# The way from attention into the experts: first weights outside the order that is kept, gates in half steps, and a later scan

## The chip, the cores and the metric

The kernel runs on one core of a Trainium2 chip. Its engines are named as in the profile: PE (TensorE, with PEld for its weight loads), DVE (VectorE), ACT (ScalarE), POOL (GpSimd) and SP (SyncE, which here only issues DMAs). The metric is the device time of one execution in microseconds (us).

## The reference

An attention with a mask from clusters, and a layer of eight experts behind it, whose gates are made by eight rounds of row and column normalisation. Cut to what matters (4 batches, 8 heads, 768 positions of 64; 3072 tokens of 512, 8 experts with 1024 hidden columns):

```python
# attention
q_assign = argmax(q_n @ c_n.T); k_assign = argmax(k_n @ c_n.T)
scores = where(q_assign[:, None] == k_assign[None, :], scale * q @ k.T, -1e9)
attn = exp(scores - max(scores)); attn = attn / (sum(attn) + 1e-9)
x = attn @ v                      # (4, 8, 768, 64) -> (3072, 512)
# experts
P = exp(x @ w_gate - max(x @ w_gate))
for _ in range(8):
    P /= P.sum(1, keepdims=True) + 1e-9
    P /= P.sum(0, keepdims=True) + 1e-9
    P *= N / E
for e in range(E):
    out += P[:, e:e + 1] * (maximum(x @ w1[e], 0) @ w2[e])
```

## The kernel before

**Attention** works through 32 pairs of a batch and a head. Each is a set of generator processes that ask a `Planner` for an engine and a time; the planner simulates the engines with estimated durations and writes the instructions out in the order of its simulated times. Its `LATENCY` and the estimates in the `yield` lines decide that order. `keep_order()` (L76) then pins it: each instruction traced so far gets an edge to the one before it on its engine, so that the scheduler cannot move it. `self.last` holds the last pinned instruction per engine, and the next one is tied to it.

When a batch is complete, `out_batch(b)` (L916) stores its transposed output `xT` to `xd[b]` in memory (L918), and makes the gates' logits `lg` (L935 to L951). For batch 0 it also reduces `xT` to its largest entry `amx` (L286) and makes from it the power of two by which the experts' input is scaled (`input_scale`, its helper's lines L238 to L269); that scale is `sx`. Late in attention the inputs of batch 0 are loaded as four quarters `xqB` and split into two float16 parts, `xs` (L300 on ACT, L303 on DVE).

**The experts** are 128 items: four batches by eight experts by four quarters of the hidden columns (`NP2` = 4). The items of batch 0 come first, then the other batches; t counts the items. An item's first layer is seven products (m = 0 to 6) of six matmuls each (L1181), combined on DVE (u and c, L1209; hl, L1197) and ACT (L1194, L1214). The second layer (L1249 to L1251, o_ps) runs one item late, between the products. In the loop over m, single steps of other generators are issued behind each product: `sink` (the gates), `scanning`, `inputs` (the next batch's input), `making` (the weights), and the loop pins the order of it all with `keep_order()` at each m.

- `load_raw(idx)` (L1074, L1078) loads a quarter of an expert's w1 and w2, two tiles of 512 KB. `make_w` scales them on ACT (L1087, L1098), forms four sums and differences (L1096), casts to float16 on ACT (L1101, L1104, L1107) and subtracts for the low part (L1102, L1105, L1108), on POOL, for item 0 on DVE. During batch 0 the made weights `wa` and `wb` are stored to `wd` (L1113, L1114), and the other batches load them from there (L1119, L1120).
- `gates()` (L1022): largest logit over all (L1025, a transpose, L1030, then a matmul with ones at L1033), exp (L1036), then eight rounds. A round is the row sums (L1039 to L1042), the column sums (L1044), a yield, a matmul with ones over the partitions (L1047) and the division (L1049 to L1052).
- `scan(e)` takes the largest entry of the next expert's weights: eight loads of 512 KB into two tiles (L279, L283) and eight reductions (L286), of which each issues the load after the next. The weights' scale comes from it. The scan of expert 0 lies in attention.
- `next_x(b)`: the four `xqB` loads of the next batch (L1152), the four maxima (L286 again), the scale (L238 to L269), differences on POOL (L296), and splitting.

PE, DVE, ACT and POOL each take their instructions in order, and SP issues the DMAs in order: one that waits for its tile holds up those behind it.

Of the kernel before, what the change touches and what calls it, by code (L numbers as in the profile page):

```python
# [8 lines left out]
F32 = mybir.dt.float32  # L9
# [5 lines left out]
ALU = mybir.AluOpType  # L15
# [43 lines left out]
class Planner:  # L59
# [93 lines left out]
def attn_moe_kernel(  # L153
# [154 lines left out]
    with ExitStack() as actx:  # L308
# [607 lines left out]
        def out_batch(b):  # L916
            yield SP, 0.625
            nc.sync.dma_start(out=xd[b], in_=xts[b])  # L918
            ev["stored", b].set(plan, plan.copied(4.4))
            if b == 0:  # L920
                yield DVE, 3.3
                largest(amx, xts[b].rearrange("p c s -> p (c s)"))
                yield t_x
                yield from input_scale(b, amx, misc_tile, sm)
                t_x.put(plan)
                ev["xmax"].set(plan)

            NG, N = NT // 2, 2 * P
            yield t_x
            for c in range(NC):  # L930
                yield PE, 0.47, 0.107, 0.43
                if c == 0:
                    ps = misc_tile()
                for g in range(NG):
                    nc.tensor.matmul(  # L935
                        ps[g * Q : (g + 1) * Q, 0:N], wg[:, c, :], xts[b][:, c, g * N : (g + 1) * N], start=(c == 0), stop=(c == NC - 1)
                    )
            ev["batch", b].set(plan)
            yield DVE, 0.335
            gt = sm.tile([NG * Q, N], F32, name="gt", bufs=1)  # L940
            nc.vector.tensor_copy(gt, ps[0 : NG * Q, 0:N])
            t_x.put(plan)
            yield t_x
            yield PE, 0.25, 0.107, 0.1
            ps = misc_tile()
            for i in range(2):
                nc.tensor.transpose(
                    out=ps[:, i * NG * Q : (i + 1) * NG * Q], in_=gt[:, i * P : (i + 1) * P], identity=ident[0 : NG * Q, 0 : NG * Q]
                )
            yield DVE, 0.1  # L950
            nc.vector.tensor_copy(  # L951
                lg[:, b * NT : (b + 1) * NT, :].rearrange("p (g i) e -> p i g e", i=2),
                ps[:, 0 : 2 * NG * Q].rearrange("p (i g e) -> p i g e", i=2, e=Q)[:, :, :, 0:E],
            )
            t_x.put(plan)
# [67 lines left out]
    def gates():  # L1023
# [11 lines left out]
        nc.vector.tensor_scalar(out=gneg, in0=ps[:, 0:1], scalar1=-1.0, scalar2=None, op0=ALU.mult)  # L1035
        nc.scalar.activation(pr, lg, AF.Exp, bias=gneg)  # L1036
        for it in range(8):
            r = gs.tile([P, NTT], F32, name="rsum")
            nc.vector.tensor_reduce(out=r, in_=pr, axis=AX, op=ALU.add)  # L1039
            nc.vector.tensor_scalar(out=r, in0=r, scalar1=1e-9, scalar2=None, op0=ALU.add)  # L1040
# [5 lines left out]
            ps = h_tile()  # L1046
            nc.tensor.matmul(ps[:, 0:E], ones, c, start=True, stop=True)  # L1047
# [3 lines left out]
            nc.vector.tensor_scalar(out=c2, in0=c2, scalar1=float(B * S) / E, scalar2=None, op0=ALU.mult)
            nc.vector.tensor_tensor(out=pr, in0=pr, in1=c2.unsqueeze(1).broadcast_to([P, NTT, E]), op=ALU.mult)  # L1052


# [26 lines left out]
    def make_w(idx, wt, by=nc.gpsimd):  # L1081
# [22 lines left out]
        nc.scalar.copy(wa[:, 0, 3:7], S_)  # L1104
        by.tensor_tensor(out=wa[:, 1, 3:7], in0=S_, in1=wa[:, 0, 3:7], op=ALU.subtract)  # L1105
        yield
        nc.scalar.copy(wb[:, 0], r2)  # L1107
        by.tensor_tensor(out=wb[:, 1], in0=r2, in1=wb[:, 0], op=ALU.subtract)  # L1108
        yield

    def store_w(idx, wt):
        fa, fb = flat(*wt)
# [33 lines left out]
    def next_x(b):  # L1146
# [5 lines left out]
            nc.sync.dma_start(out=xq[o], in_=xd[b][:, k * KC : (k + 1) * KC, j * HB : (j + 1) * HB])  # L1152
        yield
        yield
        for i, o in enumerate(XQ):
            largest(am4[:, i : i + 1], xq[o].rearrange("p c s -> p (c s)"))
            yield
        for t, a, c in LESS["T2"]:
            less(t, a, c, nc.gpsimd)
        am = gs.tile([P, 1], F32, name="am")  # L1160
        nc.vector.tensor_reduce(out=am, in_=am4, axis=AX, op=ALU.max)
        for _ in input_scale(b, am, h_tile, gs):
            yield
        for o in XS:
            if o == "B21":
                for t, a, c in LESS[o]:
# [126 lines left out]

    made = {}
    begins = {begin(i): i for i in range(NI)}
    scan_at = {1: 0, 2: 2 * NP2 - 1, **{e: 2 * NP2 * (e - 1) - NP2 - 1 for e in range(3, E)}}
    sink, scanning, making, inputs = gates(), iter(()), iter(()), iter(())
    before = iter(())
    accs = {}
    load_raw(0)  # L1300
    load_raw(1)
    wt = made[0] = w_tiles(True)
    for _ in make_w(0, wt, nc.vector):
        pass
    t = 0
    for n, (b, e) in enumerate(order):
        if e == 0:
# [4 lines left out]
        for f2 in range(NP2):  # L1312
# [19 lines left out]
            hl = hp.tile([P, 2, S], F16, name="hl")  # L1332
            for m, _ in enumerate(layer1(wt, xs[b], hh, hl)):

                if m in (0, 3, 5):
                    step(sink)
                if m in (0, 3) or m in (2, 5) and 7 <= t < 11:
                    step(scanning)
                if m in (0, 2, 3, 5, 6):
                    step(inputs)  # L1340
                while rests:
                    rests.pop(0)()
# [43 lines left out]
```

## Time and profile before

| | us |
|---|---|
| median of three runs | 2471.73 |
| their range | 2467.83 to 2471.76 |
| profiled execution, its time | 2472.1 |
| its span in the trace | 2470.3 |
| mean granted PE clock | 0.99 |

The profile is one execution: the busy time of each engine, the span in 40 slices, the chain of waits that ended last, groups of equal instructions, and, from the trace behind it, windows, waits and single rows. In a row of waits stand the instruction that waited, the one whose end released it, the total, how often and the longest. Of the page's chain that ended last these are the shares by engine:

```profile
PE 87%; DVE 8%; ACT 2%; DMA 1%; issue 1%; POOL 1%; SPq 0%; ACTq 0%; DVEq 0%; POOLq 0%
```

A row of the DMA list tells who issued, how many KB each, and the queue:

```profile
r<-in_moe_w SPq DMA_DIRECT2D x64, 512.0 KB
scan<-in_moe_w SPq DMA_DIRECT2D x56, 512.0 KB
```

### The profile page before, as it was taken

To read this page: it belongs to the slowest core of one execution; us is meant where nothing else is said; L and a number is where in the kernel's file an instruction comes from. 1 tells how busy PE (TensorE), PEld (TensorE's weight loads), DVE (VectorE), ACT (ScalarE), POOL (GpSimd) and SP (SyncE) were. 2 spreads that over 40 slices of the span, in tenths; PEclk is the share of its full clock that TensorE was granted. 3 is DMA by queue.
4 is the path that set the end of the run, shared out by engine and by line. 5 is a ranking of instruction groups with operands and counts; after the bars stand their busy time and mean duration, and the time that the engine had idled before them with its cause. 6 is when DMAs were issued, how large, how long until landed. Compare 5 with 4: busy or idle time off the path is not lost.

```text
span 2470.3 us, 32700 instructions
## 1 busy us (share of the span) xinstructions
PE 2380.3 (96%) x12848; PEld 1274.8 (52%) x12848; DVE 1360.9 (55%) x2372; ACT 834.8 (34%) x1608; POOL 668.6 (27%) x712
## 2 busy tenths in 40 slices
PE   7999999966999999999999999999999999999999
PEld 4555655533545555555555555555555555555554
DVE  7888888847555454545454445544444444444444
ACT  4555555543243333333333323222121222122121
POOL 5776777734053333222222221000000000000000
PEclk9999999988999999999999999999999999999999
DMA  6545465243356353536352334222322222222322
GB/s 145 117 104 117 106 151 137 72 171 134 122 212 240 148 185 139 198 128 218 114 211 105 134 133 157 95 94 95 113 98 94 94 106 106 94 95 99 113 103 90
DMA packets 154681, 320.29 MB, mean 130 GB/s; under 512 B 61088, under 2 KB 90528, under 8 KB 154016
## 3 DMA queue, kind: packets, MB, share of 16 engines
q1 hardware_dynamic: 154528, 318.21, 39.2%
q8 instruction: 101, 1.65, 0.3%
q14 instruction: 52, 0.43, 0.1%
HBM read 230.74 MB, written 58.72 MB: 117 GB/s over the span
## 4 chain that ended last, share of the span: by engine, by line
PE 87%; DVE 8%; ACT 2%; DMA 1%; issue 1%; POOL 1%; SPq 0%; ACTq 0%; DVEq 0%; POOLq 0%
PE h_ps L1181 34%; PE o_ps L1251 13%; PE o_ps L1249 13%; PE o_ps L1250 13%; PE av_ps L820 4%; PE max_ps L693 3%; PE exp_ps L761 2%; PE exp_ps L762 2%; DVE mrt L697 2%; DVE hl L1197 1%; PE misc_ps L553 1%; DVE vsum L503 1%; POOL psum L787 0%; DVE am L286 0%; ACT pe L768 0%
## 5 line engine op out<-in xcount | busy, mean ns | idle before, releaser
L1181 PEld LDWEIGHTS <-wa 128*128 128x128 f16 x5376 | 527.0, 98 | 454.5 <-issue 22.0
L1181 PE MATMUL h_ps<-xsT,wa 128*128 128x384 f16 x3072 | 584.7, 327 | 9.5 <-DVE gm L240 4.8
L1251 PE MATMUL o_ps<-wb,hl 128*128 128x512 f16 x1536 | 584.4, 380 | 8.9 <-DVE hl L1197 8.9
L1197 DVE SCALAR_TENSOR_TENSOR hl<-c,hh 128x384 f16<-128x384 f32 x512 | 312.0, 609 | 509.5 <-ACT hh L1194 509.3
L1250 PE MATMUL o_ps<-wb,hh 128*128 128x512 f16 x1536 | 584.4, 380 | 0.0
L1249 PE MATMUL o_ps<-wb,hh 128*128 128x512 f16 x1536 | 584.3, 380 | 0.0
L1194 ACT ACTIVATE hh<-c 128x384 f16<-128x384 f32 x512 | 267.6, 523 | 921.8 <-DVE c L1209 914.2
L1181 PE MATMUL h_ps<-xsB,wa 128*128 128x384 f16 x2304 | 420.8, 328 | 10.8 <-ACT wa L1101 7.1
L1251 PEld LDWEIGHTS <-hl 128*128 128x128 f16 x1536 | 150.5, 98 | 194.5 <-DVE hl L1197 13.3
L1209 DVE SCALAR_TENSOR_TENSOR c<-h_ps,u 128x384 f32<-128x384 f32 x256 | 142.0, 555 | 180.2 <-PE h_ps L1181 180.2
L1209 DVE SCALAR_TENSOR_TENSOR u<-h_ps,m 128x384 f32<-128x384 f32 x256 | 142.4, 556 | 171.8 <-PE h_ps L1181 171.4
L787 POOL TENSOR_TENSOR psum<-psum,pe 128x512 f32<-128x512 f32 (+1 forms) x203 | 221.6, 1109 | 48.3 <-ACT pe L768 41.8
L1096 POOL TENSOR_TENSOR r<-r 128x256 f32<-128x256 f32 x124 | 88.7, 736 | 511.7 <-ACT r L1087 509.3
L1249 PEld LDWEIGHTS <-hh 128*128 128x128 f16 x1536 | 151.1, 98 | 139.5 <-issue 1.0
L1250 PEld LDWEIGHTS <-hh 128*128 128x128 f16 x1536 | 150.3, 98 | 139.8 <-issue 1.0
L1214 ACT ACTIVATE c<-h_ps 128x384 f32<-128x384 f32 x128 | 62.7, 490 | 440.5 <-PE h_ps L1181 440.5
L697 DVE TENSOR_REDUCE mrt<-max_ps 128x1 f32<-128x512 f32 (+1 forms) x288 | 190.0, 683 | 37.0 <-PE max_ps L693 35.0
L768 ACT ACTIVATE pe<-exp_ps 128x512 f32<-128x512 f32 x288 | 165.6, 597 | 84.3 <-PE exp_ps L762 78.1
L1269 DVE SCALAR_TENSOR_TENSOR acc<-o_ps,gates,acc 128x512 f32<-128x512 f32 x168 | 125.4, 747 | 40.4 <-PE o_ps L1251 40.3
L820 PE MATMUL av_ps<-pe,vn 128*64 128x512 f32 (+1 forms) x768 | 136.3, 498 | 0.0
L693 PE MATMUL max_ps<-kX,qX 96*128 96x256 f32 (+1 forms) x384 | 126.8, 393 | 6.9 <-DVE mrt L697 4.2
L762 PE MATMUL exp_ps<-qX,kX 98*128 98x512 f32 (+1 forms) x384 | 127.9, 346 | 0.0
(199 smaller groups left out, 1915.0 us busy)
## 6 DMA issues: line engine op xcount, KB each, us to landing
wa<-wd SPq DMA_DIRECT2D x96, 896.0 KB
wb<-wd SPq DMA_DIRECT2D x96, 512.0 KB
r<-in_moe_w SPq DMA_DIRECT2D x64, 512.0 KB
wd<-wa SPq DMA_DIRECT2D x32, 896.0 KB
scan<-in_moe_w SPq DMA_DIRECT2D x56, 512.0 KB
wd<-wb SPq DMA_DIRECT2D x32, 512.0 KB
qn<-in_q SPq DMA_DIRECT2D x16, 384.0 KB
kn<-in_k SPq DMA_DIRECT2D x16, 384.0 KB
```

The lines of the kernel that those rows point to most:

```text
L693: nc.tensor.matmul(ps[:, y * (z - a) : (y + 1) * (z - a)], t["qa"][0:96, i * P : (i + 1) * P], t["k2"][0:96, a:z], start=True, stop=True)
L697: nc.vector.tensor_reduce(out=t["mr"][:, i0 : i0 + ni, ni - 1], in_=ps.rearrange("p (x c) -> p x c", x=ni), axis=AX, op=ALU.max)
L762: nc.tensor.matmul(o, t["k2"][0:98, ki], t["qa"][0:98, a:z], start=False, stop=True)
L787: (nc.gpsimd if e == POOL else nc.vector).tensor_tensor(out=st[:, a:z], in0=old[a], in1=part, op=ALU.add)
L820: nc.tensor.matmul(av[o, a:z], vn[:, i, :], heads[t]["pe", c][:, i - i0], start=(i == 0), stop=False, skip_group_check=True)
L1181: nc.tensor.matmul(ps[:, 0:HB], wa[:, w_, a, c, :], x[:, x_, c, :], start=(first and s_ == 0), stop=(s_ == len(steps) - 1), skip_group_che ...
L1194: nc.scalar.activation(hh[:, 2 - i, o], src, AF.Relu)
L1197: nc.vector.scalar_tensor_tensor(out=hl[:, 2 - i, o], in0=src, scalar=0.0, in1=hh[:, 2 - i, o], op0=ALU.max, op1=ALU.subtract)
L1209: nc.vector.scalar_tensor_tensor(out=t, in0=ps[:, 0:HB], scalar=KAPPA, in1=x, op0=ALU.mult, op1=ALU.add)
L1249: nc.tensor.matmul(po[i], hh[:, t, ti], wbh[:, t], start=(first and t == 0), stop=False)
L1250: nc.tensor.matmul(po[i], hh[:, t, ti], wbl[:, t], start=False, stop=False)
L1251: nc.tensor.matmul(po[i], hl[:, t, ti], wbh[:, t], start=False, stop=(last and t == 1))
```

## The change

1. `Planner.unpin()` is new: it forgets the last pinned instructions. It is called after the first loads of weights, the making of item 0's weights and four steps of the gates have been written out. These instructions get no edge to the end of attention; the scheduler places them where their data allow.
2. Item 0's weights are made by a function of their own, `make_first`, with casts and subtractions in wider pieces, all on ACT and DVE.
3. Batch 1 gets its maximum and scale in attention as batch 0 does (`if b < 2` in `out_batch`), and `next_x` leaves both out for it.
4. The gates yield twice a round, and are stepped at m = 0, 1, 3, 4. Their last multiplication (L1051) is folded into the addition ahead of it.
5. The scan of expert 1 begins at item 3 (it was item 0), with one step at its m = 6, three steps in item 4 and five each in items 5 and 6; until item 11 it takes four steps an item.
6. `make_w` yields twice more ahead of its last cast; the inputs of batch 1 are stepped three times an item.

```diff
+    def unpin(self):
+        self.last, self.traced = {}, len(self.instructions())
...
-            if b == 0:
+            if b < 2:
                 yield DVE, 3.3
                 largest(amx, xts[b].rearrange("p c s -> p (c s)"))
                 yield t_x
                 yield from input_scale(b, amx, misc_tile, sm)
...
         for it in range(8):
+            yield
             r = gs.tile([P, NTT], F32, name="rsum")
...
-            nc.vector.tensor_scalar(out=c2, in0=ps[:, 0:E], scalar1=1e-9, scalar2=None, op0=ALU.add)
+            nc.vector.tensor_scalar(out=c2, in0=ps[:, 0:E], scalar1=1e-9, scalar2=float(E) / (B * S), op0=ALU.add, op1=ALU.mult)
             nc.vector.reciprocal(c2, c2)
-            nc.vector.tensor_scalar(out=c2, in0=c2, scalar1=float(B * S) / E, scalar2=None, op0=ALU.mult)
...
+    def make_first(wt):
+        r1, r2 = raws.pop(0)
...
+        def parts(o, a):
+            nc.scalar.copy(wa[:, 0, o], a)
+            nc.vector.tensor_tensor(out=wa[:, 1, o], in0=a, in1=wa[:, 0, o], op=ALU.subtract)
...
+        nc.scalar.activation(raw, raw, AF.Copy, scale=s1[:, 0:1])
+        parts(slice(A11, A12 + 1), A[:, 1])
...
+        nc.scalar.activation(r2, r2, AF.Copy, scale=s2[:, 0:1])
+        nc.scalar.copy(wb[:, 0], r2)
+        nc.vector.tensor_tensor(out=wb[:, 1], in0=r2, in1=wb[:, 0], op=ALU.subtract)
...
-        for i, o in enumerate(XQ):
-            largest(am4[:, i : i + 1], xq[o].rearrange("p c s -> p (c s)"))
-            yield
+        if b >= 2:
+            for i, o in enumerate(XQ):
+                largest(am4[:, i : i + 1], xq[o].rearrange("p c s -> p (c s)"))
+                yield
...
-    scan_at = {1: 0, 2: 2 * NP2 - 1, **{e: 2 * NP2 * (e - 1) - NP2 - 1 for e in range(3, E)}}
+    scan_at = {1: NP2 - 1, 2: 2 * NP2 - 1, **{e: 2 * NP2 * (e - 1) - NP2 - 1 for e in range(3, E)}}
...
-    for _ in make_w(0, wt, nc.vector):
-        pass
+    make_first(wt)
+    step(sink, 4)
+
+    plan.unpin()
+    ANY = (0, 2, 3, 5, 6)
...
-                if m in (0, 3, 5):
+                if m in (0, 1, 3, 4):
                     step(sink)
-                if m in (0, 3) or m in (2, 5) and 7 <= t < 11:
+                if m in (((6,), (0, 3, 6), ANY, ANY)[t - NP2 + 1] if NP2 - 1 <= t < 2 * NP2 - 1 else (0, 2, 3, 5) if t < 11 else (0, 3)):
                     step(scanning)
-                if m in (0, 2, 3, 5, 6):
+                if m in ((2, 5, 6) if f2 else (4, 5, 6)) if b == 0 else m in ANY and f2 * 7 + m > 0:
                     step(inputs)
```

The line numbers of the changed kernel are larger: 4 more in attention, 5 more in the gates and the weights, and 35 to 38 more from `store_w` on. Three places show how the instructions now stand.

SP's queue, from the last pair's moves in attention (kL, qX, kX and qL are tiles of keys and queries) to the first stores of made weights. Before:

```order
L639 DMA kX_174<-ot 16x768
L733 DMA qX_153<-mt 1x6x128 x2
L741 DMA nht_206<-mt 1x6x128 x2
L733 DMA qX_170<-mt 1x6x128 x2
L741 DMA nht_206<-mt 1x6x128 x2
L918 DMA xd_89<-xT 128x3072
L1074 DMA r_6183<-in_moe_w 128x4x256
L1078 DMA r_6185<-in_moe_w 128x2x512
L1074 DMA r_6187<-in_moe_w 128x4x256
L1078 DMA r_6189<-in_moe_w 128x2x512
L1113 DMA wd_6150<-wa 128x3584
```

Now:

```order
L643 DMA kX_174<-ot 16x768
L652 DMA kL_150<-kX_156 64x768
L652 DMA qL_162<-qX_170 64x768
L1079 DMA r_6198<-in_moe_w 128x4x256
L1083 DMA r_6200<-in_moe_w 128x2x512
L737 DMA qX_153<-mt 1x6x128 x2
L745 DMA nht_206<-mt 1x6x128 x2
L737 DMA qX_170<-mt 1x6x128 x2
L745 DMA nht_206<-mt 1x6x128 x2
L1148 DMA wd_6165<-wa 128x3584
L1149 DMA wd_6165<-wb 128x2048
L1079 DMA r_6202<-in_moe_w 128x4x256
```

Item 0's two raw loads moved from behind the store of the last batch (xd_89) to behind the last pair's moves, ahead of the last masks (mt); the store of the made weights moved up with them.

ACT at attention's end and in front of the first product. Before:

```order
L768 ACTIVATE pe<-exp_ps 128x512 x10
L840 COPY xT<-av_ps 128x512
L840 COPY xT<-av_ps 128x256
L864 COPY sc<-misc_ps 128x384
L886 CAST rr<-rs 128x12 x3
L896 COPY rt<-misc_ps 36x128
L1087 ACTIVATE r_6183<-r_6183,s_96 128x1024
L1098 ACTIVATE r_6185<-r_6185,s_97 128x1024
L1101 CAST wa<-r_6183 128x256
L1101 CAST wa<-r_6183 128x512
L1104 CAST wa<-r_6183 128x1024
```

Now:

```order
L772 ACTIVATE pe<-exp_ps 128x512 x10
L1127 CAST wa<-r_6198 128x512 x3
L1127 CAST wa<-r_6198 128x256
L1143 CAST wb<-r_6200 128x1024
L844 COPY xT<-av_ps 128x512
L844 COPY xT<-av_ps 128x256
L868 COPY sc<-misc_ps 128x384
L890 CAST rr<-rs 128x12 x3
L900 COPY rt<-misc_ps 36x128
L1041 ACTIVATE pr<-lg,gneg 128x192
```

The casts of item 0's weights now stand between the last exps and the copies of the attention's output; their scaling (L1133, L1142) stands some 30 rows further up, between exps. Behind the end of attention comes the gates' exp. On DVE the subtractions (L1128, L1144) stand likewise ahead of the last normalisation, and the rows behind the last logits are these. Before:

```order
L951 COPY lg<-misc_ps 128x2x3x8
L1096 TENSOR_TENSOR r_6183<-r_6183 128x256 x4
L1102 TENSOR_TENSOR wa<-r_6183,wa 128x256
L1102 TENSOR_TENSOR wa<-r_6183,wa 128x512
L1105 TENSOR_TENSOR wa<-r_6183,wa 128x1024
L1108 TENSOR_TENSOR wb<-r_6185,wb 128x1024
L1025 TENSOR_REDUCE gmax<-lg 128x1
L1209 SCALAR_TENSOR_TENSOR u_6255<-h_ps,m_6225 128x384
L1197 SCALAR_TENSOR_TENSOR hl<-c_6264,hh 128x384
L1209 SCALAR_TENSOR_TENSOR u_6278<-h_ps,m_6225 128x384
L1030 TENSOR_REDUCE g_6282<-h_ps 1x1
L286 TENSOR_REDUCE am_6234<-xqB_6235 128x1
```

Now:

```order
L956 COPY lg<-misc_ps 128x2x3x8
L1030 TENSOR_REDUCE gmax<-lg 128x1
L1035 TENSOR_REDUCE g_6228<-h_ps 1x1
L1040 TENSOR_SCALAR gneg<-h_ps 128x1
L1045 TENSOR_REDUCE rsum<-pr 128x24
L1046 TENSOR_SCALAR rsum<-rsum 128x24
L1047 RECIPROCAL rsum<-rsum 128x24
L1048 TENSOR_TENSOR pr<-pr,rsum 128x192
L1050 TENSOR_REDUCE csum<-pr 128x8
L1055 TENSOR_SCALAR csum_6264<-h_ps 128x8
L1056 RECIPROCAL csum_6264<-csum_6264 128x8
L1057 TENSOR_TENSOR pr<-pr,csum_6264 128x192
```

The gates' first steps follow the logits at once, with their first round ahead of the first combination of products; the reduction of `xqB` is gone.

SP's queue around items 3 to 7, with the scan's loads among the loads of made weights (`wa`, `wb` from `wd`). Before:

```order
L279 DMA scan_6570<-in_moe_w 128x1024
L283 DMA scan_6648<-in_moe_w 128x2x512
L1113 DMA wd_6153<-wa 128x3584
L1114 DMA wd_6153<-wb 128x2048
L1119 DMA wa<-wd_6150 128x3584
L1120 DMA wb<-wd_6150 128x2048
L279 DMA scan_6762<-in_moe_w 128x1024
L283 DMA scan_6823<-in_moe_w 128x2x512
L1119 DMA wa<-wd_6151 128x3584
L1120 DMA wb<-wd_6151 128x2048
L1119 DMA wa<-wd_6152 128x3584
L1120 DMA wb<-wd_6152 128x2048
```

Now:

```order
L1154 DMA wa<-wd_6165 128x3584
L1155 DMA wb<-wd_6165 128x2048
L283 DMA scan_6840<-in_moe_w 128x1024
L287 DMA scan_6842<-in_moe_w 128x2x512
L1154 DMA wa<-wd_6166 128x3584
L1155 DMA wb<-wd_6166 128x2048
L283 DMA scan_6912<-in_moe_w 128x1024
L287 DMA scan_6966<-in_moe_w 128x2x512
L1154 DMA wa<-wd_6167 128x3584
L1155 DMA wb<-wd_6167 128x2048
L283 DMA scan_6985<-in_moe_w 128x1024
L287 DMA scan_7020<-in_moe_w 128x2x512
```

Before, three of the four pairs of scan loads were issued ahead of the first load of made weights; now all four come behind it.

More of the change, by code (lines that the diff above doesn't have):

```diff
@@ L925, in out_batch @@
                 t_x.put(plan)
-                ev["xmax"].set(plan)
+                if b == 0:
+                    ev["xmax"].set(plan)
             NG, N = NT // 2, 2 * P
@@ L1106, in make_w @@
         yield
+        yield
+        yield
         nc.scalar.copy(wb[:, 0], r2)
@@ L1109, in make_w, with sum_ @@
         yield
+    def make_first(wt):
+        r1, r2 = raws.pop(0)
+        wa, wb = wt
+        raw = r1[:, 0 : 4 * KC * P]
+        A = raw.rearrange("p (k c t f) -> p t k c f", k=2, c=KC, t=2)
+        S_ = r1[:, 4 * KC * P :].rearrange("p (o c f) -> p o c f", o=4, c=KC)
+        def parts(o, a):
+            nc.scalar.copy(wa[:, 0, o], a)
+            nc.vector.tensor_tensor(out=wa[:, 1, o], in0=a, in1=wa[:, 0, o], op=ALU.subtract)
+        def sum_(o, a, b_, op):
+            nc.vector.tensor_tensor(out=S_[:, o], in0=a, in1=b_, op=op)
+        nc.scalar.activation(raw, raw, AF.Copy, scale=s1[:, 0:1])
+        parts(slice(A11, A12 + 1), A[:, 1])
+        sum_(0, A[:, 0, 0], A[:, 0, 1], ALU.add)
+        sum_(1, S_[:, 0], A[:, 1, 0], ALU.subtract)
+        parts(slice(S1, S2 + 1), S_[:, 0:2])
+        sum_(2, A[:, 1, 0], A[:, 0, 0], ALU.subtract)
+        sum_(3, A[:, 1, 1], S_[:, 1], ALU.subtract)
+        parts(slice(S3, S4 + 1), S_[:, 2:4])
+        parts(A22, A[:, 0, 1])
+        nc.scalar.activation(r2, r2, AF.Copy, scale=s2[:, 0:1])
+        nc.scalar.copy(wb[:, 0], r2)
+        nc.vector.tensor_tensor(out=wb[:, 1], in0=r2, in1=wb[:, 0], op=ALU.subtract)
     def store_w(idx, wt):
@@ L1154, in next_x @@
         yield
-        for i, o in enumerate(XQ):
-            largest(am4[:, i : i + 1], xq[o].rearrange("p c s -> p (c s)"))
-            yield
+        if b >= 2:
+            for i, o in enumerate(XQ):
+                largest(am4[:, i : i + 1], xq[o].rearrange("p c s -> p (c s)"))
+                yield
         for t, a, c in LESS["T2"]:
             less(t, a, c, nc.gpsimd)
[L1160 to L1163, printed above, removed]
+        if b >= 2:
+            am = gs.tile([P, 1], F32, name="am")
+            nc.vector.tensor_reduce(out=am, in_=am4, axis=AX, op=ALU.max)
+            for _ in input_scale(b, am, h_tile, gs):
+                yield
+        yield
         for o in XS:
```

## The prediction

> **What bounds the kernel now.** I read first the page's 40 slices of the span: each is 61.8 us, each digit the busy share (or the granted clock) in tenths.
>
> ```profile
> PE   7999999966999999999999999999999999999999
> PEclk9999999988999999999999999999999999999999
> ```
>
> TensorE (PE) sets the time nearly everywhere. Only the slices from 494 to 618 us, where attention ends and the experts begin, show a 6, and there the granted clock falls as well. So I cut that place into windows; the columns are the window, its length, busy time (and instructions) of PE, PEld, DVE, ACT and POOL, then the granted clock, the DMA share and GB/s.
>
> ```profile
> 420.00:480.00 60.00, 57.68 (x345) 34.26 (x346) 51.80 (x89) 33.62 (x72) 44.83 (x50) 1.00 0.41 109
> 513.00:525.00 12.00, 7.73 (x54) 3.25 (x50) 2.32 (x7) 2.17 (x7) 1.21 (x3) 0.72 0.36 122
> 525.00:540.00 15.00, 6.80 (x32) 3.56 (x33) 7.17 (x13) 10.33 (x14) 4.36 (x6) 0.77 0.78 271
> 540.00:560.00 20.00, 10.18 (x47) 5.03 (x45) 10.67 (x25) 5.41 (x8) 7.27 (x7) 0.74 0.81 288
> 560.00:580.00 20.00, 13.04 (x55) 5.87 (x53) 13.37 (x29) 4.76 (x8) 10.33 (x7) 0.83 0.40 137
> 580.00:600.00 20.00, 14.97 (x72) 7.75 (x72) 16.40 (x36) 8.34 (x12) 8.27 (x7) 0.90 0.20 68
> 600.00:620.00 20.00, 12.27 (x55) 6.00 (x56) 16.51 (x31) 7.19 (x11) 5.69 (x3) 0.84 0.51 183
> 640.00:700.00 60.00, 60.00 (x322) 31.30 (x320) 28.18 (x54) 19.92 (x34) 15.68 (x15) 1.00 0.44 160
> ```
>
> From 513 to 620 PE is busy 7.73 + 6.80 + 10.18 + 13.04 + 14.97 + 12.27 = 65.0 us of 107: 42 us are idle. Busy time times clock, from 540 on, is 42.1 of 50.5 us: another 8.3 us go to the low clock. At most some 50 us are to be had in all, and from 640 on nothing. The third view is what PE waited for from 513 to 620 (total us, times, longest):
>
> ```profile
> PE h_ps L1047 <- DVE c L1209: 10.1, 4, 5.4
> PE h_ps L1033 <- DVE c L1209: 9.2, 1, 9.2
> PE h_ps L1181 <- ACT wa L1101: 7.1, 1, 7.1
> PE h_ps L1181 <- DVE gm L240: 4.8, 1, 4.8
> PE h_ps L1181 <- DVE g L1030: 1.3, 1, 1.3
> PE h_ps L248 <- DVE gd L245: 1.1, 1, 1.1
> ```
>
> Four rows of it, 31.2 us, are what the change is about.
>
> **The first weights.** Timeline rows (start, duration, engine, line, work, in brackets the idle time ahead):
>
> ```profile
> 459.69 0.59 SPq L639 DMA_DIRECT2D kX<-ot  x1
> 510.63 1.08 ACT L768 ACTIVATE pe<-exp_ps 128x512 f32<-128x512 f32 x2 [0.41 <-PE exp_ps L762]
> 514.33 0.86 ACT L840 COPY xT<-av_ps 128x512 f32<-128x512 f32 x2 [2.62 <-PE av_ps L828]
> 516.28 0.17 DVE L871 SCALAR_TENSOR_TENSOR rs<-misc_ps,flags 128x12 f32<-128x12 f32 x1 [3.01 <-PE misc_ps L868]
> 520.87 0.38 SPq L1074 DMA_DIRECT2D r<-in_moe_w  x1
> 524.74 0.21 DVE L951 COPY lg<-misc_ps 128x48 f32<-128x48 f32 x1 [0.48 <-PE misc_ps L947]
> 528.43 1.15 ACT L1087 ACTIVATE r<-r,s 128x1024 f32<-128x1024 f32 x1 [9.80 <-DMA r<-in_moe_w]
> 531.77 0.50 PE L1181 MATMUL h_ps<-xsB,wa 128*128 128x384 f16 x1 [7.07 <-ACT wa L1101]
> ```
>
> The weights of item 0 are issued at 520.87, after attention's last store, land at 528.43, and are scaled and split until 531.77. In the changed order these loads follow the last pair's moves (the last of them here at 459.69), some 50 us ahead of attention's end, and scaling stands between exps; only casts and subtractions stand behind the last exp. So the 7.1 us go. What is late next is the gates' start: their largest logit, once needed later (the 1.3 us on L1030), now stands before the first product. That wait changes place; I book it at nothing. The tail costs something. ACT ends its exps at 511.71 and would idle until 514.33; the casts (three of 512 columns, one of 256, one of 1024: about 3.3 us by the rows below) end near 515.0, 0.7 us into the copies of xT. DVE's subtractions follow the casts; the last, 1024 columns wide (twice 0.69), ends near 516.4, inside the same delay of the sum at 516.28. **−7.1, +0.7.** If the early scaling waited for its load it would stop the exps, but the queue has some 10 us for 1 MB while the DMA share is 0.41.
>
> ```profile
> L1101 ACT CAST wa<-r x2: 389/500/612, 530.8 to 531.1; 128x256 f16<-128x256 f32 x1, 128x512 f16<-128x512 f32 x1
> L1107 ACT CAST wb<-r x1: 1041/1041/1041, 532.6 to 532.6; 128x1024 f16<-128x1024 f32 x1
> L1102 DVE TENSOR_TENSOR wa<-r,wa x2: 425/560/694, 531.2 to 531.7; 128x256 f16<-128x256 f32 x1, 128x512 f16<-128x512 f32 x1
> ```
>
> (The three numbers are least, median and largest ns.)
>
> **Batch 1's maximum.** The 9.2 us are one event:
>
> ```profile
> 547.13 0.95 DVE L286 TENSOR_REDUCE am<-xqB 128x1 f32<-128x768 f32 x1 [8.28 <-DMA xqB<-xd]
> 550.22 0.58 PE L1033 MATMUL h_ps<-g,ones 1*128 1x1 f32 x2 [9.20 <-DVE c L1209]
> ```
>
> DVE stood 8.28 us at the first maximum of batch 1's input, issued behind 1.5 MB of weights and scan tiles; combinations of products queued behind it, PE behind those. The change takes the four maxima (and the scale, on which the 4.8 and 1.1 us hang) out of the experts and makes them one reduction inside attention. The gates' first step moves ahead of the products, so nothing there stands behind this load. **−9.2, −4.8, −1.1.** The tiles are still loaded, for splitting, but no scan load stands ahead of them any more; I allow up to 3 us of a new wait for them in the range.
>
> The price inside attention is read where batch 0 does the same:
>
> ```profile
> 184.04 3.35 DVE L286 TENSOR_REDUCE amx<-xT 128x1 f32<-128x3072 f32 x1
> 184.00:192.00 8.00, 7.97 (x49) 4.77 (x48) 6.57 (x9) 5.91 (x12) 6.43 (x7) 1.00 0.81 261
> ```
>
> PE lost 0.03 us there: the cover is PE's queue of pairs. But attention as a whole is planned anew with it, and DVE is at 51.80 of 60 us late in attention, with ACT now scaling raw weights too. If the cover fails the reduction costs 3.35 us, with the small steps 5. **+1**, range 0 to 5.
>
> **The gates and DVE's load.** What DVE does between 534 and 640 (group: count, busy us, mean ns, idle before):
>
> ```profile
> L286 DVE TENSOR_REDUCE am<-scan 128x1 f32<-128x1024 f32 x8 | 9.7, 1208 | 0.0
> L286 DVE TENSOR_REDUCE am<-xqB 128x1 f32<-128x768 f32 x4 | 3.8, 943 | 8.3 <-DMA xqB<-xd 8.3
> L1051 DVE TENSOR_SCALAR csum<-csum 128x8 f32<-128x8 f32 x8 | 2.2, 279 | 0.3
> ```
>
> PE's wait at L1047 is for a column sum queued on DVE behind the previous whole iteration, a scan reduction and a maximum, in stretches where DVE is 82% busy (16.40 and 16.51 of 20). Now 9.7 (scan, to later items), 3.8 (maxima), 2.2 (folded multiply) and about 1.3 us (the scale's small steps) leave, 17 us in all, and each step is half as long. I take 7 of the 10.1 as gone (bounds 0 and 10.1): one of its four waits, 5.4 us, is over half of it, and I expect about one short wait per item to stay, some 3 us together. A stall remains too: the first iteration's column sum now stands between the first two products, while DVE needs about 4.5 us from the last logits to it and PE only about 3.5. **−7, +1.**
>
> **The clock.** With most of the long waits gone the 8.3 us shrink. Item 0 stays cold, since the short steps ahead of it ran at 0.72. I take **−5**, bounds 0 and 8.3.
>
> [...] If many short waits hold the clock down as well, they may do so after the change, and the sum without this term is 2449.7 us.
>
> **The scan.** It starts at item 3, takes up to five steps an item, and has two tiles: each next load is issued only after a reduction has freed its tile, behind 1.4 MB of made weights per item on the queue. The price of such a wait shows where the next expert's scan runs against those loads:
>
> ```profile
> 699.13 1.22 DVE L286 TENSOR_REDUCE am<-scan 128x1 f32<-128x1024 f32 x1 [4.17 <-DMA scan<-in_moe_w]
> 700.00:710.00 10.00, 7.17 (x37) 3.42 (x36) 8.82 (x14) 4.96 (x7) 3.29 (x3) 1.00 0.52 184
> 710.00:760.00 50.00, 48.71 (x261) 25.24 (x259) 24.28 (x46) 22.13 (x36) 26.04 (x23) 1.00 0.60 224
> ```
>
> 4.17 us of DVE cost PE up to 2.83 + 1.29 = 4.1 us (10 and 50 less their busy times). With two tiles, three further pairs of loads can meet this: none (0) to three (12.4). I take one, **+4.1**.
>
> **Sum** against the profiled run (2472.1 us, span 2470.3; the median of the shown runs, 2471.73, stands 0.4 lower): −7.1 − 9.2 − 4.8 − 1.1 − 7 − 5 = −34.2; +0.7 + 1 + 1 + 4.1 = +6.8; net −27.4, so 2444.7 us.
>
> **The rivals.**
>
> *DVE stays the bound, held by POOL (chance 0.20).* In these rows DVE's multiplication took 1.89 us, ending as POOL's work ended, against a least of 0.357 (in the last row: least, median, largest ns of the eight):
>
> ```profile
> 566.61 1.89 DVE L1042 TENSOR_TENSOR pr<-pr,rsum 128x192 f32<-128x192 f32 x1
> 566.17 2.11 POOL L1105 TENSOR_TENSOR wa<-r,wa 128x1024 f16<-128x1024 f32 x1
> L1042 DVE TENSOR_TENSOR pr<-pr,rsum x8: 357/358/1886, 552.6 to 616.1; 128x192 f32<-128x192 f32 x8
> ```
>
> The same POOL work pressed into fewer us meets the gates more often; half steps don't help. Then L1047's 10.1 and the clock's 8.3 stay: net −27.4 + 12 = −15.4, 2456.7 us. Against it: 17 us of other work leave DVE. [...]
>
> *The scan starves at all three pairs (0.12):* −27.4 + 8.3 = −19.1, 2453.0 us.
>
> *Slower (0.05):* the scan's loads form a chain. What is left of it is emptied at the end of item 6, and then each pair waits a whole landing: 8.28 us was DVE's wait on such a queue, times four pairs is 33.1. With a cold clock after each (the 5 us given back) that is −27.4 − 4.1 + 33.1 + 5 = +6.6: 2478.7 us. It decides where the steps come faster than about 8 us a pair; items of about 15 us with five steps each come near that only in items 5 and 6. For it speaks the 4.17 us wait; against it that PE lost nothing more there.
>
> *The change does not do what it says (0.05):* the first weights' early loads find no free tile and land where they did. Then 7.1 us stay and the tail's 0.7 go: −21.0, 2451.1 us.
>
> **How the numbers follow.** The forecast has 0.55, the rivals 0.42, and 0.03 is left for gains beyond its bounds. Its largest gain takes all of L1047's wait and of the clock's loss, none for the scan, and nothing for attention and the first column sum: −27.4 − 3.1 − 3.3 − 4.1 − 2 = −39.9, 2432. Upward the range takes in the first rival, with the 5 us for attention in place of 1 and 2 of the 3 us for the input tiles: 2456.7 + 4 + 2, 2463. Left out are the slower case and what lies beyond these sums, under 2 in 10. A difference of 0.2% (4.9 us) is about what a measurement of this kernel can tell from no change. Faster by more: 0.88; within: 0.06, from rivals whose costs add; slower: 0.06.
>
> **What would show it.** Right: PE's first product within 3 us of the last logits; no maxima of xqB for batch 1 and no wait of DVE on them; PE idle from attention's end to item 4 down from 42 us to about 15; clock over 0.9 from 40 us after attention's end. Wrong: attention's last exp later than 511.7 by several us, waits at the gates' matmul above 5 us in total, or DVE waits on scan loads in items 4 to 6 beyond 5 us.

## The result and the profile after

| | before | changed |
|---|---|---|
| median, us (six runs each) | 2471.60 | 2447.11 |
| range, us | 2467.83 to 2471.76 | 2442.95 to 2453.28 |
| profiled execution, its time, us | 2472.1 | 2450.72 |
| its span, us | 2470.3 | 2448.7 |

The ratio is 0.9905 with an interval of 0.9889 to 0.9922: 24.5 us by the medians, 21.4 us by the two profiled executions. The forecast of 2444.7 us is 2.4 us off. The rest of this part shows that several of its terms were not where it put them.

The page's slices of the changed kernel (61.2 us each):

```profile
PE   7999999978999999999999999999999999999999
PEclk7999999989999999999999999999999999999999
```

The dent is shallower, not gone. The windows around it, with the columns of before:

```profile
525.00:540.00 15.00, 11.92 (x51) 5.34 (x51) 6.57 (x20) 3.08 (x5) 2.97 (x4) 0.50 0.95 335
540.00:560.00 20.00, 14.67 (x69) 7.64 (x68) 13.70 (x26) 9.39 (x15) 12.86 (x10) 0.80 0.35 124
560.00:580.00 20.00, 16.16 (x89) 8.48 (x88) 15.48 (x29) 10.92 (x18) 11.35 (x9) 1.00 0.33 117
580.00:600.00 20.00, 14.84 (x70) 7.08 (x69) 16.67 (x27) 5.87 (x10) 9.92 (x6) 0.91 0.23 91
600.00:620.00 20.00, 19.62 (x106) 10.28 (x105) 12.58 (x24) 4.65 (x9) 0.00 (x0) 1.00 0.54 205
```

PE idles 3.1 + 5.3 + 3.8 + 5.2 + 0.4 = 17.8 us of 95 here. Its waits from 500 to 620:

```profile
PE h_ps L1219 <- DVE csum L1055: 7.8, 7, 3.1
PE h_ps L1219 <- DVE c L1247: 4.7, 1, 4.7
PE misc_ps L897 <- ACT rr L890: 2.5, 1, 2.5
PE h_ps L1053 <- DVE c L1247: 2.5, 2, 1.7
```

The rows of 9.2, 7.1 and 4.8 us are gone; what stays are products behind the gates on DVE. Two timeline rows, the last exps of attention and the first product:

```profile
515.52 1.08 ACT L772 ACTIVATE pe<-exp_ps 128x512 f32<-128x512 f32 x2 [0.41 <-PE exp_ps L766]
532.38 2.10 PE L1219 MATMUL h_ps<-xsB,wa 128*128 128x384 f16 x6
```

Attention's last exp ends at 516.60, 4.9 us later than before. The first product starts at 532.38 with no wait for weights, 0.6 us later than the 531.77 of before. So nothing was gained up to there in this execution.

Where the time did come from shows when each item is timed by ACT's copy of its first product (m<-h_ps, one row an item: L1214 before, L1252 now):

| item | before | changed | ahead by |
|---|---|---|---|
| 0 | 533.90 | 534.52 | −0.6 |
| 1 | 555.78 | 553.01 | 2.8 |
| 2 | 583.22 | 573.24 | 10.0 |
| 3 | 612.64 | 595.54 | 17.1 |
| 4 | 628.74 | 610.57 | 18.2 |
| 13 | 766.15 | 749.78 | 16.4 |
| 42 | 1198.72 | 1176.06 | 22.7 |
| 61 | 1478.78 | 1453.13 | 25.6 |
| 70 | 1612.49 | 1591.06 | 21.4 |
| 127 | 2444.41 | 2422.97 | 21.4 |

From item 0 to item 4 the changed kernel gains 18.8 us. From 4 to 13 it gives back 1.8. From 13 to 61 it gains 9.2, which the forecast had not seen; from 61 to 70 it loses 4.2, not seen either.

**Items 4 to 6** are where the late scan now runs. DVE's waits for its loads from 590 to 660 us, of which there are none there before:

```profile
DVE am L290 <- DMA scan<-in_moe_w: 6.2, 3, 2.5
```

**Items 13 to 61.** The gain comes in steps of about 1.6 us, one per eight items (the first four by items 18, 26, 34 and 42). The rows around the first step: before, POOL's subtraction for wb lies beside DVE's hl, and PE waits for hl:

```profile
838.76 2.12 POOL L1108 TENSOR_TENSOR wb<-r,wb 128x1024 f16<-128x1024 f32 x1 [4.22 <-ACT wb L1107]
839.14 2.15 DVE L1197 SCALAR_TENSOR_TENSOR hl<-c,hh 128x384 f16<-128x384 f32 x1 [2.24 <-ACT hh L1194]
841.36 0.39 PE L1251 MATMUL o_ps<-wb,hl 128*128 128x512 f16 x1 [1.37 <-DVE hl L1197]
```

Now the same subtraction comes after the last hl of the item:

```profile
823.40 0.56 DVE L1235 SCALAR_TENSOR_TENSOR hl<-c,hh 128x384 f16<-128x384 f32 x1 [0.59 <-ACT hh L1232]
824.38 2.12 POOL L1115 TENSOR_TENSOR wb<-r,wb 128x1024 f16<-128x1024 f32 x1 [6.19 <-ACT wb L1114]
```

hl takes 0.56 in place of 2.15 us. Two edits are candidates: the two further yields in `make_w`, which were called a part of the change and given no price, and the moved scan.

**Items 61 to 70** are where the input of batch 2 is made ready. PE's busy time of 1440 to 1640, before and now:

```profile
1440.00:1640.00 200.00, 198.96 (x1063) 103.70 (x1062) 102.85 (x182) 51.70 (x95) 14.95 (x8) 1.00 0.33 121
```

```profile
1440.00:1640.00 200.00, 195.52 (x1040) 101.06 (x1038) 105.60 (x183) 50.82 (x94) 16.30 (x8) 1.00 0.35 126
```

### The profile page after: what moved, and what is told of

It reads as the page before. It is cut to its first block, busy times and chain, and to the rows that moved or that the text cites. A ratio compares the mean times of both kernels' runs of the same rounds, so it can differ in the third digit from the quotient of the medians.

```text
span 2448.7 us, 32683 instructions
## 1 busy us (share of the span) xinstructions
PE 2383.3 (97%) x12848; PEld 1275.6 (52%) x12848; DVE 1342.4 (55%) x2354; ACT 836.1 (34%) x1616; POOL 672.4 (27%) x712
## 4 chain that ended last, share of the span: by engine, by line
PE 86%; DVE 7%; issue 3%; ACT 2%; DMA 1%; POOL 0%; SPq 0%; POOLq 0%; ACTq 0%; DVEq 0%
PE h_ps L1219 34%; PE o_ps L1289 13%; PE o_ps L1287 13%; PE o_ps L1288 13%; PE av_ps L824 4%; PE max_ps L697 3%; PE exp_ps L765 2%; DVE mrt L701 2%; PE exp_ps L766 2%; DVE vsum L507 1%; PE misc_ps L557 1%; DVE hl L1235 1%; PE misc_ps L861 0%; ACT pe L772 0%; PE misc_ps L940 0%
## 5 line engine op out<-in xcount | busy, mean ns | idle before, releaser
L1235 DVE SCALAR_TENSOR_TENSOR hl<-c,hh 128x384 f16<-128x384 f32 x512 | 291.0, 568 | 493.1 <-ACT hh L1232 492.6
L791 POOL TENSOR_TENSOR psum<-psum,pe 128x512 f32<-128x512 f32 (+1 forms) x207 | 227.2, 1115 | 54.2 <-ACT pe L772 46.6
L1287 PEld LDWEIGHTS <-hh 128*128 128x128 f16 x1536 | 151.0, 98 | 139.2 <-issue 0.6
L1252 ACT ACTIVATE c<-h_ps 128x384 f32<-128x384 f32 x128 | 62.7, 490 | 424.7 <-PE h_ps L1219 424.7
```

The lines of the kernel that those rows point to most:

```text
L791: (nc.gpsimd if e == POOL else nc.vector).tensor_tensor(out=st[:, a:z], in0=old[a], in1=part, op=ALU.add)
L1235: nc.vector.scalar_tensor_tensor(out=hl[:, 2 - i, o], in0=src, scalar=0.0, in1=hh[:, 2 - i, o], op0=ALU.max, op1=ALU.subtract)
L1287: nc.tensor.matmul(po[i], hh[:, t, ti], wbh[:, t], start=(first and t == 0), stop=False)
```

## The experiments

Each kernel was timed beside the kernel before on the same chip, and its ratio is to those runs. The changed kernel, whose ratio is 0.9905, was not timed again beside them. Stretches between items, such as the way from the first product to item 4 (76.1 us in the changed kernel), are read from one profiled execution each.

**1. The two further yields alone** (in the kernel before, `make_w`):

```diff
         yield
+        yield
+        yield
         nc.scalar.copy(wb[:, 0], r2)
```

> The kernel before with the two further yields in make_w alone. Theory: in the changed kernel PE's waits for hl at the second layer fell from 8.9 us to 1.4 us because the low part of wb is now subtracted on POOL after the last combination of products, and no longer beside DVE's hl, which it held to 2.15 us instead of 0.56. Then this edit alone takes 5 to 8 us: 2464 to 2467 us beside 2471.6, and PE's waits for hl fall below 3 us. Rival: those waits fell because of the later scan or the new steps elsewhere; then 2471 us and 8 to 9 us of waits for hl.

Measured: 2466.73 us, 0.9978 (0.9966 to 0.9989), 5.4 us by the ratio. The row of waits for hl after 640 us, which was 8.9 us:

```profile
PE o_ps L1253 <- DVE hl L1199: 0.4, 2, 0.2
```

**2. The changed kernel without them.**

> The changed kernel without the two further yields in make_w. Theory (POOL beside DVE): 5 to 8 us slower than the changed kernel, 2452 to 2455 us, and the waits for hl are back at 8 to 9 us. Rival (other parts did it): 2447 us.

Measured: 2462.95 us, 0.9964 (0.9952 to 0.9977), and the wait is back:

```profile
PE o_ps L1287 <- DVE hl L1233: 10.0, 9, 1.4
```

In its table of items it is 16.3 us ahead of before at item 13 and still 16.3 at item 61, where the changed kernel is at 25.6. The yields did it: all the kernels here that have them take 703.4 us from item 13 to item 61 (704.9 in kernel 5), and all that lack them 712.6. They also cost something earlier. From item 4 to item 13 kernel 1 takes 140.1 us and the kernel before 137.4, the changed kernel 139.2 and this one 138.0. The ratios differ by 14.6 us (0.9964 − 0.9905), twice what was expected, the two profiled executions by 9.7; what the larger difference holds beside the yields stays open.

**3. Batch 1's maximum back among the experts** (in the changed kernel; input steps as before):

```diff
-            if b < 2:
+            if b == 0:
...
-        if b >= 2:
+        if b >= 1:
...
-                if m in ((2, 5, 6) if f2 else (4, 5, 6)) if b == 0 else m in ANY and f2 * 7 + m > 0:
+                if m in ANY:
```

> The changed kernel with batch 1's maximum and scale back among the experts (five input steps an item, as before). The prediction's theory: DVE waits on the xqB load again and PE behind it, up to 9.2 + 4.8 + 1.1 = 15 us, less the 1 us put down for attention: about 2461 us, with a wait of DVE on xqB of several us. Rival 1: with no scan loads ahead of them the tiles land in time, so only the maxima's own 5 us on DVE come back: 2447 to 2452 us. On attention's end, 4.9 us later in the changed kernel's profile: if the new plan with the maximum causes it, the last exp ends near 511.7 us here; if PE's low clock of that execution causes it, it does so only where the clock holds.

Measured: 2439.69 us, 0.9873 (0.9858 to 0.9888): faster than the changed kernel, where the forecast's theory wanted it 14 us slower and the rival up to 5. DVE does not wait for xqB, and the first product to item 4 takes 76.2 us, in the changed kernel 76.1. Beside the other edits the maximum in attention bought nothing. The kernel's lead is elsewhere: of 11.7 us between the two profiled executions 8.5 are there at attention's end and 3.0 come from items 61 to 70, with the old input steps.

**4. Without unpin:**

```diff
-    plan.unpin()
```

> The changed kernel without the call of unpin: item 0's loads, making and the gates' first steps stay behind attention's end. The prediction's theory: the 7.1 us before the first product come back, less the 0.7 us of the tail: 2453 to 2455 us, and PE waits about 7 us for the first weights. Rival: the first product is held by late logits and cold clock anyway, or later items absorb it: 2447 to 2449 us.

Measured: 2458.86 us, 0.9946 (0.9933 to 0.996), some 10 us more than the changed kernel. The wait is larger than the 7.1 us of before, since the gates' first steps, now written ahead of the first product, wait on DVE behind the making of the weights:

```profile
PE h_ps L1033 <- DVE gmax L1030: 13.9, 1, 13.9
```

The first product's copy comes 29.8 us after the last exp, in the changed kernel 17.9. The rival (absorbed later) falls.

From the first product to item 4 this kernel takes 75.4 us, no more than the changed kernel. So the gain of items 0 to 3 does not need unpin. SP's queue is held here too, for 10.6 us, by the store of item 0's weights, but the first reader of xqB comes 12.8 us after the issue of its loads and does not wait:

```profile
530.54 0.34 SPq L1148 DMA_DIRECT2D wd<-wa  x1
534.98 2.58 SPq L1187 DMA_DIRECT2D xqB<-xd  x4
547.79 1.79 POOL L300 TENSOR_TENSOR tx<-xqB,xqB 128x768 f32<-128x768 f32 x1
```

Which of the other edits (no scan loads ahead of xqB, the later input steps, the maximum in attention) does this was not separated.

**5. The scan at item 0 again** (in the changed kernel):

```diff
-    scan_at = {1: NP2 - 1, 2: 2 * NP2 - 1, ...}
+    scan_at = {1: 0, 2: 2 * NP2 - 1, ...}
...
+                if m in (0, 3) or m in (2, 5) and 7 <= t < 11:
                     step(scanning)
```

> The changed kernel with the scan of expert 1 begun at item 0 again, and with its steps as before. Beside the changed kernel's 0.9905 of the kernel before. The prediction's theory: eight reductions of 1.21 us return to the items in which DVE is the bound, and the scan's loads stand ahead of others on the queue, while items 4 to 9 no longer lose the 1.9 us they lost: net some 3 to 8 us slower than the changed kernel, 0.992 to 0.994. Rival: the products' pace in items 0 to 3 is set by the cold clock and by POOL, not by DVE's sum of work: no difference or up to 2 us faster, 0.990. Attention is the same program as in the changed kernel: if PE's low clock near 440 to 465 us belongs to that order, it is here too and the last exp ends near 516 us; if to the execution, it need not be.

Measured: 2443.68 us, 0.9889 (0.9876 to 0.9901). No slower, as the rival had it; 75.9 us from the first product to item 4. Its reason, a pace set by the cold clock and by POOL, is not shown by this; what is shown is that DVE has a place for the scan here.

**6. Whole steps of the gates** (in the changed kernel):

```diff
         for it in range(8):
-            yield
...
-    step(sink, 4)
+    step(sink, 3)
...
-                if m in (0, 1, 3, 4):
+                if m in (0, 3, 5):
                     step(sink)
```

> The changed kernel with whole steps of the gates (no yield at a round's start, three steps ahead of unpin, stepped at m = 0, 3, 5 as before; the folded multiplication stays). The prediction's theory: the waits at the gates' matmul that fell from 10.1 to 3.1 us return in part: 4 to 8 us slower than the changed kernel, 0.992 to 0.994. Rival: those waits had been DVE's maxima and scan, not the size of a step: within 2 us of the changed kernel, 0.9905.

Measured: 2444.40 us, 0.9891 (0.9877 to 0.9905), 76.9 us from the first product to item 4. The waits at the gates' matmul did return (8.7 us in three), but others went, and no loss of time shows.

**7. Batch 1's maximum in attention alone** (in the kernel before): the two edits of `out_batch` and `next_x`.

```diff
-            if b == 0:
+            if b < 2:
                 yield DVE, 3.3
...
+        if b >= 2:
             for i, o in enumerate(XQ):
                 largest(am4[:, i : i + 1], xq[o].rearrange("p c s -> p (c s)"))
```

> The kernel before with batch 1's maximum and scale taken in attention, nothing else. The prediction's terms for this edit: 9.2 + 4.8 + 1.1 us of waits go, 1 us comes in: 2458 us beside 2472, 0.994. Rival, from the kernel with this edit taken out, which was not slower: the waits move to the next thing that DVE or PE lacks, and less than 5 us are gained, 0.998 or more.

Measured: 2467.51 us, 0.9985 (0.9977 to 0.9994): 3.7 us in place of 14, as the rival had it. The long wait stays, on another reader of the same load. ACT's row, DVE's behind it and PE's behind that:

```profile
554.80 0.93 ACT L300 ACTIVATE xsB<-xqB,sx 128x768 f16<-128x768 f32 x1 [7.99 <-DMA xqB<-xd]
555.77 1.02 DVE L303 SCALAR_TENSOR_TENSOR xsB<-xqB,sx,xsB 128x768 f16<-128x768 f32 x1 [8.45 <-ACT xsB L300]
559.38 0.58 PE L1034 MATMUL h_ps<-g,ones 1*128 1x1 f32 x2 [9.91 <-DVE c L1212]
```

The maximum was only the first to read the late tiles. With it gone, the split, the next on that tile, waits 8.0 us, where the maximum had waited 8.28.

**8. Unpin alone** (in the kernel before): `make_first` in place of `make_w(0, ...)`, three whole steps of the gates, unpin.

```diff
-    for _ in make_w(0, wt, nc.vector):
-        pass
+    make_first(wt)
+    step(sink, 3)
+    plan.unpin()
```

> The kernel before with unpin, the new making of item 0's weights and three whole steps of the gates written ahead of it, nothing else. The prediction's terms: the 7.1 us before the first product go, 0.7 comes in, and the gates' first matmul no longer stands behind DVE's wait for xqB (a part of the 9.2 us): 2458 to 2466 us, 0.994 to 0.9975. If this edit by itself undoes most of the waits for xqB too (the rival to the term for batch 1's maximum): 0.993 or less.

Measured: 2459.43 us, 0.9948 (0.9936 to 0.9959): 12.9 us, at the far end of what was expected. The profiled execution is 13.7 us ahead of the kernel before at item 4: 3.6 us of it at attention's end, 5.4 from there to the first product's copy, 4.8 from there to item 4. DVE's first maximum of xqB does not wait:

```profile
537.99 0.49 DVE L1048 TENSOR_REDUCE csum<-pr 128x8 f32<-128x192 f32 x1
538.40 0.94 DVE L290 TENSOR_REDUCE am<-xqB 128x1 f32<-128x768 f32 x1
```

So unpin alone also takes away the wait for xqB. SP issues its DMAs in the program's order here: in the kernel before, it stood for 9.1 us from 524.7 us on at the store of item 0's weights, until they were made, with xqB's loads behind:

```profile
533.95 0.34 SPq L1113 DMA_DIRECT2D wd<-wa  x1
539.51 2.34 SPq L1152 DMA_DIRECT2D xqB<-xd  x4
```

With the weights made in attention the queue runs on, and xqB's loads are issued at 526.88 us, 11.5 us ahead of the first maximum. The wait of 4.8 us for batch 1's scale stays, at 5.0.

**9. Input steps of batches 2 and 3 from the first product on** (in the changed kernel):

```diff
-                if m in (... if f2 else ...) if b == 0 else m in ANY and f2 * 7 + m > 0:
+                if m in (... if f2 else ...) if b == 0 else m in ANY:
                     step(inputs)
```

> The changed kernel with the input steps of batches 2 and 3 taken from the first product of the first quarter on, as before (the further yield in next_x stays). Near 1490 to 1530 us the changed kernel loses 4.2 us against the kernel before, and the kernel without batch 1's maximum, which also had the old steps, only 0.7. Theory: the steps do it, one place later they meet other work of DVE: about 3 us faster than the changed kernel, 0.989 to 0.9895 of the kernel before. Rival: something else in that kernel did, or the execution: 0.9905 and the same loss. The attention is that of the changed kernel: the last exp comes near 509.5 us where the clock stays full and near 516 where it falls between 440 and 465 us.

Measured: 2441.14 us, 0.9876 (0.9863 to 0.989). Items 61 to 70 take 134.8 us, in the changed kernel 137.9 and before 133.7, so the steps do cost about 3 us there. Of the profiled execution's lead of 9.6 us the greater part, 7.2, is there at attention's end already. The loss near 1500 us is mostly gone:

```profile
1440.00:1640.00 200.00, 198.00 (x1058) 103.34 (x1057) 106.11 (x185) 51.90 (x96) 11.25 (x6) 1.00 0.33 116
```

**10 to 12. Two and three of DVE's loads back.** Kernels 3, 5 and 6 each put back one of the edits that relieve DVE in items 0 to 3, and none cost anything. Here the edit of 3 is joined with that of 5, that of 6, and both.

> The kernel without batch 1's maximum in attention, and with the scan back at item 0; half steps stay. Theory (DVE's work in items 0 to 3 decides, and any one of its three loads may stay but not two or three): the way from the first product to item 4 goes from 76 us to 80 to 90, 5 to 12 us slower than without the maximum alone (0.9873): 0.989 to 0.992. Rival (what made 90 us of it with unpin alone was something else, the order of DVE's queue): 76 to 78 us, 0.9873 to 0.988.

> The kernel without batch 1's maximum in attention, and with whole steps of the gates; the scan stays late. Theory (DVE's work): as for the scan, but half steps take no work away, so 76 to 80 us from the first product to item 4, 0.9873 to 0.989. Rival (the length of a step decides once maxima stand between): 80 to 90 us, 0.989 to 0.992.

> The same with all three back: maximum among the experts, scan at item 0, whole steps of the gates; unpin and the further yields stay. If effects add: unpin alone 0.9948 and the yields alone 0.9978 give 0.9926, and about 90 us from the first product to item 4. If the three loads on DVE do not matter: 0.9873 to 0.988.

| put back, or edit alone | first product to item 4, us | ratio to before |
|---|---|---|
| nothing (the changed kernel) | 76.1 | 0.9905 |
| nothing, without unpin (4) | 75.4 | 0.9946 |
| maximum (3) | 76.2 | 0.9873 |
| scan (5) | 75.9 | 0.9889 |
| whole steps (6) | 76.9 | 0.9891 |
| maximum and scan (10) | 82.7 | 0.9892 (0.9876 to 0.9908) |
| maximum and whole steps (11) | 81.1 | 0.9889 (0.9875 to 0.9902) |
| all three (12) | 88.1 | 0.9912 (0.9897 to 0.9927) |
| unpin alone (8) | 90.0 | 0.9948 |
| batch 1's maximum in attention alone (7) | 90.7 | 0.9985 |
| the kernel before | 94.8 | 1 |

The first column leaves out where attention ends, which moves from execution to execution, and is the steadier of the two. Any one of the three may stay; a second beside the maximum costs 5 to 6.5 us and the third 5.4 to 7, about 12 in all. The scan and the whole steps together, without the maximum, were not run. In 10 and 12 the expected direction came out. In 11 it is on the line between the two theories: whole steps take no work from DVE, and still cost 4.9 us once the maxima stand between them, as the rival had it. It is room on DVE that they share, whether as work or as the length of one step; which of the two it is was not separated.

## Why the prediction came out right

The forecast was within 2.4 us, and its range held. That it came so near is partly luck: terms that were too large and terms that were missing nearly cancelled. PE's idle time from 513 to 620 us fell from 42 us to about 21.5, where about 15 had been forecast. By its own steps:

- **The first weights (−7.1, +0.7).** Right in mechanism. From attention's last exp to the first product's copy it was 22.2 us before and is 17.9 now, −4.3; the last logits end 0.84 us later after the last exp than before, 0.7 having been forecast. The gates' first steps, booked at nothing, take the rest: the first product starts 2.0 us after the last logits' matmul. What the term left out is that unpin moves SP's whole queue, with xqB behind it: in kernel 8 a further 4.8 us came between the first product and item 4. With the other edits in place that part is not needed (kernel 4).
- **Batch 1's maximum (−9.2, −4.8, −1.1).** The step that failed. The waits went, but this edit was not what they needed: alone it gives 3.7 us (kernel 7), and taking it out costs nothing beside the other edits (kernel 3), where the load is there in time. The prediction took the instruction that waited for the cause, though it had noted what stood ahead of the load (by the rows of SP's queue four loads of 512 KB, 2 MB and not 1.5, and ahead of them the store that held the queue); a wait on data that is late stays with the next reader. It allowed up to 3 us for that reader, and with this edit alone 8.0 stayed.
- **Its price in attention (+1).** Right in size, about 1.2 us. The last exp ends at 509.3 to 509.6 us with the maximum (kernels 5, 6 and 9) and at 508.1 to 508.2 without (kernels 3, 8 and 11). Left out are executions in which the clock fell between 100 and 300 us or for longer near 450 us, among them kernels 10 and 12, without the maximum, at 511.5 and 511.8 (0.83 from 240 to 260 us in both). Kernel 4, with the maximum but without the making of item 0's weights in attention, ends its exps at 507.1, so the price hangs on what else lies there.
- **The gates (−7, +1).** PE's waits at the gates' matmul fell from 10.1 to 3.1 us, the 7 that were forecast. But they moved: the products that wait for the gates' sums on DVE (csum) went from 2.1 to 7.8 us. Taking the half steps out alone costs nothing (kernel 6); beside the maxima they are worth 4.9 us. The three edits that free DVE share about 12 us between them, and were priced one by one.
- **The clock (−5).** An estimate inside the 8.3 us, which no run shows as such; in its place the windows show a gain from 540 us on, where it was counted, and a loss ahead of that. Busy time times the missing clock is 2.9 + 0 + 1.3 + 0 = 4.2 us from 540 to 620, and was 8.3. But from 525 to 540 it is 6.0, and was 1.6: item 0 began at 0.50 where 0.77 had been granted before. Over both it is 10.2 us, and was 9.9, so nothing was gained.
- **The scan (+4.1).** From item 4 to item 13 it took 137.4 us before and takes 139.2 now, but the kernel with the early scan (5) takes 140.2, and kernel 2, with the late scan and without the yields, 138.0. So the greater part of what is lost there is the yields'. DVE did wait for the scan's loads in items 4 to 6: 6.2 us in three waits, more than the 5 that the prediction had named as a sign of being wrong. PE lost little by it: items 4 to 6 take 44.7 us, and took 44.3 before. The rival of starving loads was right about DVE's waits and wrong about what they cost.
- **What was missing.** The yields in `make_w` (5.4 us alone, by ratio: 9.2 us gained between items 13 and 61, some of it lost between 4 and 13) and the input steps (about 3 us lost). Both were read as moves with no price: for the first, PE's row of 8.9 us after 640 us on the waits for hl belonged beside POOL's rows, and it was the same collision that the prediction had shown between POOL and the gates (1.89 us, median 0.358).

POOL holding DVE, the first rival's mechanism, shows in the changed kernel too, and still costs there. The longest of its waits behind the gates, 3.1 us:

```profile
580.85 2.40 POOL L300 TENSOR_TENSOR tx<-xqB,xqB 128x768 f32<-128x768 f32 x1
581.52 2.15 DVE L1235 SCALAR_TENSOR_TENSOR hl<-c,hh 128x384 f16<-128x384 f32 x1
584.26 0.97 PE L1219 MATMUL h_ps<-xsT,wa 128*128 128x384 f16 x5 [3.11 <-DVE csum L1055]
```

Here hl took 2.15 us beside POOL's difference, 1.6 more than the median of 0.56 of the 77 hl from 560 to 860 us. Two kernels with a part undone (3 and 9) are the fastest measured, 2439.7 and 2441.1 us; both have the old input steps. Kernel 3's interval ends below where that of the changed kernel begins, kernel 9's just touches it; how much of this is the clock in attention, below, was not separated.

The end of attention moves with the execution. It was one of the prediction's signs of being wrong, and it showed: the changed kernel's profiled execution ends its exps at 516.6 us, 4.9 us later than before. But kernels 5, 6 and 9, with the same attention, end them at 509.3 to 509.6 (kernel 2 at 515.6). Against kernel 5 the profiled execution lost 3.0 us by the middle of the exps and 4.2 us behind that. At both places the clock fell, first near 241 us:

```profile
240.00:248.00 8.00, 8.00 (x31) 3.52 (x31) 4.89 (x6) 3.73 (x8) 5.66 (x6) 0.57 0.27 58
```

There it stayed at 1.00 in kernel 5; in the profiled execution of the kernel before it was 0.57 as well. The second place is between 440 and 465 us:

```profile
452.00:456.00 4.00, 2.48 (x20) 1.69 (x18) 2.18 (x3) 2.18 (x5) 2.33 (x3) 0.97 0.51 106
456.00:460.00 4.00, 3.74 (x12) 1.46 (x13) 2.07 (x4) 1.71 (x4) 2.67 (x3) 0.50 0.35 68
460.00:464.00 4.00, 4.00 (x16) 1.84 (x15) 0.47 (x1) 0.00 (x0) 0.00 (x0) 0.68 0.35 71
```

The same stretch in kernel 5:

```profile
452.00:456.00 4.00, 3.96 (x22) 1.77 (x23) 2.55 (x3) 1.20 (x3) 2.25 (x3) 1.00 0.39 79
456.00:460.00 4.00, 4.00 (x23) 3.27 (x21) 3.64 (x6) 2.51 (x4) 2.36 (x2) 1.00 0.44 89
460.00:464.00 4.00, 3.91 (x21) 1.54 (x19) 3.96 (x6) 1.08 (x3) 4.00 (x5) 1.00 0.93 298
```

So of the 4.9 us by which attention ended later about 1.2 are the maximum's price, and the rest goes with the second fall of the clock, not with the new plan. Kernel 1, with the attention of before, also ended it 3.8 us later than the kernel before. Why the clock falls in one execution and not in another stays open.

## What to carry to other kernels

A wait on a load belongs to whatever made the load late: look up who stood ahead of it in its queue, and ask who reads the data next, before crediting an edit that removes the reader. An edit that costs nothing when it is taken out may still have an effect that another edit also has: test each alone as well. Edits that relieve the same engine can share one gain (about 12 us here); price them together against the point at which another engine sets the pace, not one by one. And a step that only moves needs its neighbour on the other engines looked up: two places later an operation of POOL no longer held DVE (0.56 us in place of 2.15), and that alone gave 5.4 us, where the whole change gave 24.5.

## What the runs showed of the hardware

In the changed kernel the granted clock stayed at 0.50 for 12 us in which PE was busy 72 to 92% of each 4 us:

```profile
527.00:531.00 4.00, 2.87 (x20) 0.99 (x14) 0.92 (x3) 0.00 (x0) 0.00 (x0) 0.50 1.06 391
531.00:535.00 4.00, 2.98 (x9) 1.31 (x9) 2.19 (x8) 0.94 (x3) 0.00 (x0) 0.50 0.94 320
535.00:539.00 4.00, 3.70 (x12) 1.96 (x13) 1.61 (x6) 2.08 (x3) 2.75 (x4) 0.50 1.06 377
```

So a PE that was busy for 80% of these 12 us was not granted the full clock. And the same attention program ended its exps at 509.3 us with a clock of 1.00 from 240 to 248 and from 452 to 464 us (kernel 5), and at 516.6 us with 0.57 in the first of these stretches and 0.97, 0.50 and 0.68 in the 4 us parts of the second (the changed kernel).
